# Spreading a phase's last products over the next phase's first, in a kernel of attention features and two feed-forward layers

## The chip, the cores and the metric

One core of a Trainium2 chip runs the program. The metric is the device time of one execution in microseconds. Three runs of the kernel before gave 2034.95, 2035.83 and 2037.15 us; their median is 2035.83 us. One further execution was profiled; it took 2038.37 us, of which the trace's span covers 2036.6 us.

## What is computed

```python
# attention with exponential features, then x of 2304 tokens x 512
x = np.ascontiguousarray(attn_out.transpose(0, 2, 1, 3)).reshape(B * S, H * D)
# layer 1: eight experts, all used by every token, weighted by P[:, e]
for e in range(E):                       # E = 8, w1[e] 512 x 1024, w2[e] 1024 x 512
    h = np.maximum(x @ w1[e], 0.0)
    out += P[:, e:e + 1] * (h @ w2[e])
# layer 2, on layer 1's output
h = np.maximum(np.maximum(x @ w1, x @ w2), x @ w3)      # each 512 x 768
return h @ w_out                                         # 768 x 512
```

P comes from a gate `exp(x @ w_gate)` with eight rounds of row and column normalisation. The second layer's weights arrive as 64-bit numbers and are made 32-bit on the chip ("wide" jobs).

## The kernel before

**Phases.** After the attention part the feed-forward part runs in four phases: phase 0 is layer 1 on the first half of the tokens (1152), phase 1 layer 1 on the second half, phases 2 and 3 are layer 2 on the first and the second half. A phase is a row of units of 256 hidden features: 32 units in a phase of layer 1, 3 in a phase of layer 2. A unit has one weight matrix m in layer 1 and three (m = 0, 1, 2) in layer 2. Each half has two token groups g = 0, 1 of 576 tokens.

**Products.** For each matrix and group, `group` (L304) computes the hidden block with seven products of half size. Product k multiplies a combination x0 to x6 of the input with a combination of the weight. They run in the order `PRODUCTS`, which asks for x0, x3, x4, x1, x5, x2, x6. Every product is six TensorE matmuls of 288 columns (L117 to L119), since each operand stands as a high and a low part. Three products' sums are copied from PSUM by ScalarE (u1, u5, u2: L354, L370, L374) and added on VectorE (L112, into ph or c); the third product x4 goes into the bank from which u1 was copied, x5 into the bank from which u2 was copied, x6 waits for the sum c. In layer 1 ScalarE applies the ReLU (h, L336) and VectorE makes the low part of h (L337). In layer 2 VectorE takes maxima in a tile d (L342), and with m = 2 ScalarE and VectorE write h from d (L344, L345).

**Tiles out.** `tile_out` (L386) multiplies 128 tokens of a unit's h with its second weight: six matmuls of 512 columns into a bank po or small, and one VectorE operation that adds into acc. A unit has nine tiles, t = 0 to 8. They are given between the products of the next unit's m = 0. After the last unit of a phase of layer 1, `retranspose` (L416) transposes each finished tile of acc on TensorE (four matmuls of 128 columns), ScalarE copies it (L422), and SP stores it in x_of for the phase two later.

**x jobs.** The next phase's x0 to x6 for a group are made by `x_jobs` (L133) from the group's x: four differences t3 to t6, seven high parts xh (ScalarE casts, L109), seven low parts xl (L112). `X_PLANS["between"]` says in `on` which engine makes high, low and t (A ScalarE, D VectorE, P GpSimd), and in `rest` their order. In the last group of a phase two jobs of the next phase's group 0 are issued with each product.

**At a phase's end** (L511 to L533) tiles 0 to 3 stand between the last products, tiles 4 to 8 follow in one piece with three x jobs behind each, and only then the next phase begins. Group 0's x is loaded into d, a tile of four parts that the wide jobs and the maxima use at other times; group 1's x is loaded into a buffer of h.

**Order.** The program is written in the order in which each engine runs it: there is no scheduler, and every engine takes its instructions in that order.

Of the kernel before, what the change touches and what calls it, by code (L numbers as in the profile page):

```python
# [29 lines left out]
    "between": dict(  # L30
        on=["ADD", "APD", "APD", "ADD", "ADD", "APD", "ADD"], early="h0 l0",
        rest="t3 h3 l3 t4 h4 l4 h1 l1 t5 h5 l5 h2 l2 t6 h6 l6", first=2, side=3, mix=1, weights="AAAA PPPP DDDD",
    ),
# [21 lines left out]
def tile_performer__moe__max3(ctx, tc, kq_t, kq, v1, omega2, w_gate, w1, w2, m1, m2, m3, m_out, out):  # L55
# [76 lines left out]

    def x_jobs(xf, g, plan, on=None):  # L133


        b11, b12 = xf[:, 0:2, 0:Q], xf[:, 0:2, Q:S]
        b21, b22 = xf[:, 2:4, 0:Q], xf[:, 2:4, Q:S]
        unmade.update((g, k) for k in range(7))
# [4 lines left out]
        def job(what, k):  # L143
            hi, lo = xo[g][k]
            if what == "t":
                src[k] = big.tile([P, 2, Q], F32, tag="t", name=f"t{k}", bufs=3)
                x, y = of[k]
                return lambda: tt(on[k][2], src[k], x, src[y] if isinstance(y, int) else y, ALU.subtract)
            if what == "h":
                return lambda: copy(on[k][0], hi, src[k])  # L150

            def low():
                tt(on[k][1], lo, src[k], hi.bitcast(F32), ALU.subtract)
                unmade.discard((g, k))
            return low
# [82 lines left out]

    def d4():
        return pools["b"].tile([P, KD, S], F32, tag="d", name="d")  # L240

    def wide_jobs(i, st):
# [3 lines left out]
        high = st.bitcast(I32).rearrange("p (f w) -> p f w", w=2)[:, :, 1]  # L246
        d = d4()
        sc, ma, fr = (d[:, j, :512] for j in range(3))
        sci, mai = sc.bitcast(I32), ma.bitcast(I32)
# [198 lines left out]
    def feed_forward():  # L448
        hs, last, tiles, x_plan = {}, None, [], X_PLANS["first"]
        for a, (u, m) in enumerate(mats):  # L450
            hf, layer, n = units[u]
# [3 lines left out]
            if m == 0:  # L455
                tiles += [(last, t) for t in range(HT)] if n else []
                h = hs[u] = new_h()
                hs.pop(u - 2, None)
                if layer == 2:
                    d = d4().rearrange("p k (g q) -> p k g q", g=G)  # L460
                    most[:] = [[d[:, 2 * i + j] for j in range(2)] for i in range(2)]
            if end:
# [3 lines left out]

            def load_x(out, g):
                nc.sync.dma_start(out=out, in_=x_of[phase + 1][:, :, g * S : (g + 1) * S])
                return out

            if more and layer == 1:
                xin = [load_x(d4(), 0)]
            if layer == 2 and m == 1 and n == FF2 // UF - 1 and phase < 3:
                xf = new_h(F32)
                xin = [load_x(xf[:, :, g * S : (g + 1) * S], g) for g in range(G)]

# [10 lines left out]

            def give_tile():  # L490
                v, t = tiles.pop(0)
                tile_out(v, hs[v], t)
                if v == u and layer == 1:
                    if t:
                        retranspose(2 + hf, t - 1)
                    if t == HT - 1:
                        retranspose(2 + hf, t)

            for g in range(G):
                own = end and g == G - 1  # L500
                if own:
                    while tiles:
                        give_tile()
                    if more:
                        if layer == 1:
                            xin.append(load_x(new_h(F32)[:, :, :S], 1))
                        side.extend(x_jobs(xin[0], 0, x_plan))
                pace = len(tiles)
                for i, _ in enumerate(group(a, g, h, PRODUCTS)):
                    piece()  # L510
                    if own and i == 2:  # L511
                        tiles = [(u, t) for t in range(HT // 2)]
                        pace = 0
                    if own:
                        if i > 2:
                            give_tile()
                    else:
                        left = pace - (i + 1) * pace // (7 if end else 7 * (G - g))
                        while len(tiles) > left:
                            give_tile()  # L520
                    yield
            while run_next(jobs):
                pass
            if end:
                while waiting:
                    one_more()
                if more:
                    side.extend(x_jobs(xin[1], 1, x_plan))
                tiles = [(u, t) for t in range(HT // 2, HT)]
                while tiles:  # L530
                    give_tile()
                    for _ in range(x_plan["side"]):
                        side_job()  # L533
            last = u


    def attention(pool, proj_pool):
# [167 lines left out]
        def X(s, part):  # L705
# [16 lines left out]
            if part == 1:  # L722
                if hp == HP - 1:
                    if hf == 0:
                        todo.extend(x_jobs(xf0[:, :, o : o + S], b, X_PLANS["first"], [ON["Jhi"] + ON["Jlo"] + ON["Jsum"]] * 7))
                    if b == G:
# [195 lines left out]
```

## Time and profile before

| | us |
|---|---|
| median of three runs | 2035.83 |
| profiled execution | 2038.37 |
| its span | 2036.6 |
| PE busy | 1972.6 (97%) |
| DVE busy | 1401.9 (69%) |
| ACT busy | 810.2 (40%) |
| POOL busy | 715.1 (35%) |
| phase 0 to 1, from the last group's first product to unit 1 | 918.5 to 963.6 |
| phase 1 to 2, to unit 0's second matrix | 1690.4 to 1735.5 |
| phase 2 to 3, to unit 0's second matrix | 1852.3 to 1897.9 |

PE is TensorE's matmul queue, DVE VectorE, ACT ScalarE, POOL GpSimd. Matmuls are pipelined: one of 288 columns is shown with about 0.30 us, but the next one starts 0.13 us later. So the cost of a matmul is read from start to start, and lost time is what lies above that.

### The profile page before, as it was taken

How to read it: one execution, taken by the hardware profiler on the slowest of the kernel's cores; microseconds unless marked ns; L12 is line 12 of the kernel's file. 1: busy time of each engine (PE TensorE's matmuls, PEld its weight loads, DVE VectorE, ACT ScalarE, POOL GpSimd, SP SyncE). 2: the span in 40 equal slices, each digit the busy share in tenths (PEclk: the TensorE clock that was granted, in tenths of full speed). 3: DMA queues.
4: the chain of work that ended last, by engine and by line, in shares of the span. 5: the costliest groups of instructions: out<-in, count | busy, mean ns of one | idle time of the engine just before them, and what ended most of it. 6: DMA issues, size and time to landing. Idle time of an engine off the chain costs nothing.

```text
span 2036.6 us, 33535 instructions
## 1 busy us (share of the span) xinstructions
PE 1972.6 (97%) x12906; PEld 1765.4 (87%) x12906; DVE 1401.9 (69%) x2741; ACT 810.2 (40%) x2011; POOL 715.1 (35%) x575
## 2 busy tenths in 40 slices
PE   8999999999999999998999999999999998998899
PEld 6778889999998998987999999999898987987888
DVE  5775778788878778766666666666666666567655
ACT  6775333333333333335333333333333334433442
POOL 2452234444434444423332222333222323333530
PEclk9999999999999999999999999999999999999999
DMA  6452112222222222213111111111111113113201
GB/s 206 151 187 71 42 47 73 94 80 82 73 73 73 82 90 83 68 45 112 52 46 49 42 42 42 42 52 53 42 42 42 42 65 103 51 32 120 67 22 47
DMA packets 92545, 143.95 MB, mean 71 GB/s; under 512 B 6496, under 2 KB 48608, under 8 KB 92384
## 3 DMA queue, kind: packets, MB, share of 16 engines
q1 hardware_dynamic: 92384, 141.81, 21.4%
q8 instruction: 101, 1.65, 0.3%
q14 instruction: 60, 0.49, 0.1%
HBM read 123.70 MB, written 18.09 MB: 70 GB/s over the span
## 4 chain that ended last, share of the span: by engine, by line
PE 89%; DVE 6%; ACT 3%; issue 1%; DMA 1%; SPq 0%; DVEq 0%; ACTq 0%
PE ph L117 15%; PE ph L118 14%; PE ph L119 14%; PE po L393 9%; PE po L394 9%; PE po L392 9%; PE small L393 5%; PE small L394 5%; PE small L392 5%; PE ph L621 1%; PE ph L565 1%; DVE small L624 1%; DVE s L112 1%; ACT qp L644 1%; DVE xl L112 1%
## 5 line engine op out<-in xcount | busy, mean ns | idle before, releaser
L117 PE MATMUL ph<-xh,wh 128*128 128x288 f32 x2296 | 688.8, 300 | 26.9 <-DVE c L112 10.3
L118 PE MATMUL ph<-xl,wh 128*128 128x288 f32 x2296 | 682.6, 297 | 0.0
L119 PE MATMUL ph<-xh,wl 128*128 128x288 f32 x2296 | 678.7, 296 | 0.0
L117 PEld LDWEIGHTS ph<-xh,wh 128*128 128x128 f32 x2296 | 434.7, 189 | 61.5 <-DVE c L112 14.0
L118 PEld LDWEIGHTS ph<-xl,wh 128*128 128x128 f32 x2296 | 435.0, 189 | 25.1
L119 PEld LDWEIGHTS ph<-xh,wl 128*128 128x128 f32 x2296 | 435.9, 190 | 0.0
L410 DVE SCALAR_TENSOR_TENSOR acc<-po,prob,acc 128x512 f32<-128x512 f32 x354 | 265.0, 748 | 203.0 <-PE po L394 200.9
L112 POOL TENSOR_TENSOR w2l<-st,w2h 128x512 fp32r<-128x512 f32 x140 | 183.7, 1333 | 621.8 <-ACT w2h L109 614.6
L336 ACT ACTIVATE h<-ph 128x288 fp32r<-128x288 f32 x384 | 157.8, 412 | 447.0 <-DVE ph L112 397.7
L392 PE MATMUL po<-w2h,h 128*128 128x512 f32 x834 | 328.2, 394 | 1.9 <-ACT h L344 1.9
L394 PE MATMUL po<-w2h,h 128*128 128x512 f32 x834 | 327.8, 393 | 1.8 <-DVE h L345 1.8
L393 PE MATMUL po<-w2l,h 128*128 128x512 f32 x834 | 328.9, 394 | 0.0
L112 POOL TENSOR_TENSOR wl<-st,wh 128x512 fp32r<-128x512 f32 (+1 forms) x162 | 168.0, 1043 | 292.4 <-ACT wh L109 292.4
L112 POOL TENSOR_TENSOR wl<-s,wh 128x512 fp32r<-128x512 f32 x162 | 213.6, 1323 | 31.2 <-ACT wh L109 28.6
L410 DVE SCALAR_TENSOR_TENSOR acc<-small,prob,acc 128x512 f32<-128x512 f32 x177 | 132.9, 751 | 121.7 <-PE small L394 120.9
L394 PEld LDWEIGHTS po<-w2h,h 128*128 128x128 f32 x834 | 157.1, 188 | 38.1 <-DVE h L345 2.7
L112 DVE TENSOR_TENSOR ph<-ph,u 128x288 f32<-128x288 f32 x304 | 140.3, 462 | 70.1 <-PE ph L119 54.6
L392 PEld LDWEIGHTS po<-w2h,h 128*128 128x128 f32 x834 | 157.1, 188 | 21.5 <-ACT h L344 2.3
L337 DVE SCALAR_TENSOR_TENSOR h<-ph,h 128x288 fp32r<-128x288 f32 x384 | 171.6, 447 | 2.0 <-ACT h L336 1.0
L393 PEld LDWEIGHTS po<-w2l,h 128*128 128x128 f32 x834 | 157.0, 188 | 18.3
L393 PE MATMUL small<-w2l,h 128*128 128x512 f32 x426 | 168.3, 395 | 0.0
L392 PE MATMUL small<-w2h,h 128*128 128x512 f32 x426 | 168.3, 395 | 0.0
(167 smaller groups left out, 2456.5 us busy)
## 6 DMA issues: line engine op xcount, KB each, us to landing
st<-in_moe_w_dram SPq DMA_DIRECT2D x146, 512.0 KB, 3.6
st<-plain SPq DMA_DIRECT2D x24, 512.0 KB, 3.7
raw<-in_kq_t_dram SPq DMA_DIRECT2D x15, 576.0 KB, 4.4
sq<-in_kq_dram SPq DMA_DIRECT2D x15, 576.0 KB, 5.0
plain<-d SPq DMA_DIRECT2D x24, 256.0 KB, 2.2
v<-in_v_dram SPq DMA_DIRECT2D x16, 325.0 KB, 5.1
h<-x_of SPq DMA_DIRECT2D x4, 1152.0 KB, 6.0
x_of<-xt SPq DMA_DIRECT2D x18, 256.0 KB, 2.6
```

The costliest lines, as they stand in the source:

```text
L112: (nc.gpsimd if on == "P" else nc.vector).tensor_tensor(out=out, in0=in0, in1=in1, op=op)
L117: nc.tensor.matmul(ps, wh, xh, start=start and not onto, stop=False, **given)
L118: nc.tensor.matmul(ps, wh, xl, start=False, stop=False, **given)
L119: nc.tensor.matmul(ps, wl, xh, start=False, stop=stop, **given)
L336: after(0, lambda: nc.scalar.activation(hh, c, AF.Relu))
L337: after(1, lambda: nc.vector.scalar_tensor_tensor(out=hl, in0=c, scalar=0.0, in1=hh.bitcast(F32), op0=ALU.max, op1=ALU.subtract))
L392: nc.tensor.matmul(ps, h[:, f, ts], wh[:, f], start=f == 0, stop=False)
L393: nc.tensor.matmul(ps, h[:, f, ts], wl[:, f], start=False, stop=False)
L394: nc.tensor.matmul(ps, h[:, 2 + f, ts], wh[:, f], start=False, stop=f == 1)
L410: nc.vector.scalar_tensor_tensor(out=a, in0=ps, scalar=prob[:, i, e : e + 1], in1=a, op0=ALU.mult, op1=ALU.add)
L565: nc.tensor.matmul(o[j], w[:, j], x, start=start, stop=stop)
L621: nc.tensor.matmul(ps[h][:, i], x[d, t0 + i], om[d, h * M : (h + 1) * M], start=True, stop=True)
```

## The change

Six things change.

1. The last unit's tiles 4 to 8 are no longer given in one piece. They stay in the list `tiles`, each with the transposition of the tile two before it, and are given between the next phase's first products. In phase 1 they are spread over both groups of its first unit.
2. In layer 2 a new function `due` spreads a unit's nine tiles over all its matrices, one behind the sixth product of each group and the rest evenly; before, all nine stood in m = 0. In the last unit of phase 2 they are spread over m = 0 and 1.
3. d becomes two tiles d0 and d1 of two parts each. At the change from phase 0 to 1 group 1's x is loaded into them, half by half, by the new jobs u0 and u1, once group 0's jobs have used the half. Elsewhere group 1's x still goes into a buffer of h, in two loads.
4. The x jobs between phases come in another order (t5 earlier), and the low part of x5 is made on VectorE instead of GpSimd: nine of the eleven differences and low parts of a group are now on VectorE, before eight.
5. In layer 2 the buffer h of a unit is taken with m = 2 instead of m = 0, and the next phase's x is loaded with the last unit's m = 2 instead of m = 1.
6. The x jobs of group 0 that are left at the phase's end, and all of group 1, run between the next phase's first products.

```diff
     "between": dict(
-        on=["ADD", "APD", "APD", "ADD", "ADD", "APD", "ADD"], early="h0 l0",
-        rest="t3 h3 l3 t4 h4 l4 h1 l1 t5 h5 l5 h2 l2 t6 h6 l6", first=2, side=3, mix=1, weights="AAAA PPPP DDDD",
+        on=["ADD", "APD", "APD", "ADD", "ADD", "ADD", "ADD"], early="h0 l0",
+        rest="t3 h3 t5 l3 u0 t4 h4 l4 h1 l1 t6 h2 l2 u1 h5 l5 h6 l6", first=2, side=3, mix=1, weights="AAAA PPPP DDDD",
     ),
...
+            if what == "u":
+                return lambda: used(k)
...
-    def d4():
-        return pools["b"].tile([P, KD, S], F32, tag="d", name="d")
+    def d2(c):
+        return pools["b"].tile([P, KD // 2, S], F32, tag=f"d{c}", name=f"d{c}")
...
+        def out_of(v):
+
+
+            hf, layer, n = units[v]
+            given = [[lambda t=t: tile_out(v, hs[v], t)] for t in range(HT)]
+            if layer == 1 and n == E * FF // UF - 1:
+                given += [[], []]
+                for t in range(HT):
+                    given[t + 2].append(lambda t=t: retranspose(2 + hf, t))
+            return given
+
...
+            if layer == 1 or m == 2:
+                hs.pop(u - 2, None)
                 h = hs[u] = new_h()
...
+            def used(c):
+                if phase == 0:
+                    xin[1].append(load_x(d2(c), 1, c))
...
+            def due(g, i):
+
+                if layer == 1:
+
+                    return pace - (i + 1) * pace // (7 if end else 7 * (G - g))
+
+                groups = G * (2 if end_unit and phase < 3 else 3)
+                q = G * m + g
+                rest = max(0, total - groups)
+                return max(0, total - q - (i >= 5) - min(rest, (7 * q + i + 1) * rest // (7 * groups)))
...
                     if own and i == 2:
-                        tiles = [(u, t) for t in range(HT // 2)]
-                        pace = 0
+                        tiles = out_of(u)
                     if own:
-                        if i > 2:
-                            give_tile()
+                        if 2 < i:
+                            give()
                     else:
-                        left = pace - (i + 1) * pace // (7 if end else 7 * (G - g))
+                        left = due(g, i)
                         while len(tiles) > left:
-                            give_tile()
+                            give()
                     yield
...
                 if more:
+                    while len(xin[1]) < 2:
+                        side_job()
                     side.extend(x_jobs(xin[1], 1, x_plan))
-                tiles = [(u, t) for t in range(HT // 2, HT)]
-                while tiles:
-                    give_tile()
-                    for _ in range(x_plan["side"]):
-                        side_job()
             last = u
+        while tiles:
+            give()
```

How it moves the instructions, at three places. In the names, xh03 is the high part of x3 of group 0 and xl13 the low part of x3 of group 1; wh0 and wl0 are the weight parts of one of two slots; `acc<-po,prob,acc` is a tile's addition.

On PE, the end of phase 0 in the kernel before: tile 8's last matmuls, the transpositions of tiles 7 and 8, and phase 1's first product.

```order
L392 MATMUL small_10228<-w2h_9864,h_9849 128x512
L393 MATMUL small_10228<-w2l_9865,h_9849 128x512
L394 MATMUL small_10228<-w2h_9864,h_9849 128x512
L420 MATMUL ph_10236<-ident_66,acc_2762 128x128 x4
L420 MATMUL ph_10244<-ident_66,acc_2762 128x128 x4
L117 MATMUL ph_10260<-xh00_68,wh0_100 128x288
L118 MATMUL ph_10260<-xl00_69,wh0_100 128x288
L119 MATMUL ph_10260<-xh00_68,wl0_101 128x288
```

In the changed kernel phase 1's products x0 and x3 come right behind tile 3 and the transposition of tile 1; behind them stand tile 4, the transposition of tile 2 and product x4:

```order
L394 MATMUL po_10202<-w2h_9890,h_9873 128x512
L395 MATMUL po_10202<-w2l_9891,h_9873 128x512
L396 MATMUL po_10202<-w2h_9890,h_9873 128x512
L422 MATMUL ph_10210<-ident_66,acc_2762 128x128 x4
L117 MATMUL ph_10174<-xh04_76,wh0_100 128x288
L118 MATMUL ph_10174<-xl04_77,wh0_100 128x288
L119 MATMUL ph_10174<-xh04_76,wl0_101 128x288
```

So five tiles and seven transpositions moved from ahead of phase 1's first product to places between its first fourteen.

On DVE, the same change of phase in the kernel before: group 0's last low part, then group 1's x jobs, taken from the buffer h, with the additions of the last tiles between them.

```order
L112 TENSOR_TENSOR xl06_81<-t6_10166,xh06_80 128x576
L112 TENSOR_TENSOR xl10_83<-h_10007,xh10_82 128x576
L410 SCALAR_TENSOR_TENSOR acc_2762<-po_10188,prob_67,acc_2762 128x512
L112 TENSOR_TENSOR t3_10204<-h_10007 128x576
L112 TENSOR_TENSOR xl13_89<-t3_10204,xh13_88 128x576
L410 SCALAR_TENSOR_TENSOR acc_2762<-po_10208,prob_67,acc_2762 128x512
L112 TENSOR_TENSOR t4_10224<-h_10007,t3_10204 128x576
L112 TENSOR_TENSOR xl14_91<-t4_10224,xh14_90 128x576
```

In the changed kernel:

```order
L112 TENSOR_TENSOR xl05_79<-t5_10068,xh05_78 128x576
L112 TENSOR_TENSOR xl06_81<-t6_10147,xh06_80 128x576
L112 TENSOR_TENSOR xl10_83<-d0_10080,xh10_82 128x576
L412 SCALAR_TENSOR_TENSOR acc_2762<-po_10202,prob_67,acc_2762 128x512
L112 TENSOR_TENSOR t3_10225<-d0_10080 128x576
L112 TENSOR_TENSOR t5_10228<-d1_10168,d0_10080 128x576
L112 TENSOR_TENSOR ph_10232<-ph_10232,u1_10171 128x288
L112 TENSOR_TENSOR xl13_89<-t3_10225,xh13_88 128x576
L112 TENSOR_TENSOR t4_10242<-d1_10168,t3_10225 128x576
```

The low part of x5 joined DVE's queue, group 1's x comes from d0 and d1, and a sum of phase 1's own first products (ph with u1) now stands among group 1's jobs.

On PE in phase 2, unit 0, m = 1, first group, the kernel before: product x2 is followed at once by product x6.

```order
L117 MATMUL ph_17636<-xh02_72,wh1_2493 128x288
L118 MATMUL ph_17636<-xl02_73,wh1_2493 128x288
L119 MATMUL ph_17636<-xh02_72,wl1_2494 128x288
L117 MATMUL ph_17626<-xh06_80,wh1_2493 128x288
L118 MATMUL ph_17626<-xl06_81,wh1_2493 128x288
L119 MATMUL ph_17626<-xh06_80,wl1_2494 128x288
```

In the changed kernel a tile and a transposition stand behind product x2, ahead of x6:

```order
L394 MATMUL po_17649<-w2h_17118,h_17101 128x512
L395 MATMUL po_17649<-w2l_17119,h_17101 128x512
L396 MATMUL po_17649<-w2h_17118,h_17101 128x512
L422 MATMUL ph_17657<-ident_66,acc_2762 128x128 x4
L117 MATMUL ph_17593<-xh06_80,wh1_2493 128x288
L118 MATMUL ph_17593<-xl06_81,wh1_2493 128x288
L119 MATMUL ph_17593<-xh06_80,wl1_2494 128x288
```

So a tile of six matmuls moved into a group that had none.

## Rows read from the trace of the kernel before

**Rows 1.** The page, busy time, share of the span and instructions by engine.

```profile
PE 1972.6 (97%) x12906; PEld 1765.4 (87%) x12906; DVE 1401.9 (69%) x2741; ACT 810.2 (40%) x2011; POOL 715.1 (35%) x575
```

**Rows 2.** Stretches: length, busy of PE, PEld, DVE, ACT, POOL; TensorE clock; DMA.

```profile
600.00:800.00 200.00, 200.00 (x1173) 180.36 (x1172) 160.26 (x290) 72.02 (x171) 84.01 (x68) 1.00 0.23 76
920.00:940.00 20.00, 18.45 (x109) 15.61 (x108) 15.46 (x24) 10.21 (x20) 4.26 (x3) 1.00 0.47 152
918.50:963.60 45.10, 37.79 (x218) 33.23 (x217) 30.80 (x50) 23.36 (x49) 16.07 (x12) 0.92 0.40 126
1690.40:1735.50 45.10, 37.51 (x219) 33.28 (x218) 30.09 (x45) 21.37 (x43) 16.43 (x12) 0.92 0.40 126
1852.30:1897.90 45.60, 33.84 (x179) 29.11 (x178) 34.39 (x53) 18.25 (x38) 20.69 (x16) 0.93 0.32 99
1735.50:1852.30 116.80, 112.00 (x743) 104.90 (x743) 70.10 (x145) 47.92 (x111) 41.03 (x33) 1.00 0.18 57
1897.90:2020.00 122.10, 117.65 (x779) 110.26 (x778) 72.10 (x150) 49.38 (x115) 40.15 (x32) 1.00 0.09 27
```

**Rows 3.** Timeline of PE, phase 0 to 1: start, duration, instruction, idle before.

```profile
945.10 0.66 PE L420 MATMUL ph<-ident,acc 128*128 128x128 f32 x4 [2.26 <-DVE acc L410]
946.28 0.44 PE L117 MATMUL ph<-xh,wh 128*128 128x288 f32 x1
946.52 0.44 PE L118 MATMUL ph<-xl,wh 128*128 128x288 f32 x1
955.12 0.40 PE L117 MATMUL ph<-xh,wh 128*128 128x288 f32 x1 [2.22 <-DVE c L112]
```

**Rows 4.** Timeline of PE, starts of a transposition, products and a tile.

```profile
929.74 0.60 PE L420 MATMUL ph<-ident,acc 128*128 128x128 f32 x4
930.10 0.38 PE L117 MATMUL ph<-xh,wh 128*128 128x288 f32 x1
...
964.39 0.29 PE L117 MATMUL ph<-xh,wh 128*128 128x288 f32 x1
...
965.19 0.39 PE L392 MATMUL po<-w2h,h 128*128 128x512 f32 x1
...
966.57 0.29 PE L117 MATMUL ph<-xh,wh 128*128 128x288 f32 x1
```

**Rows 5.** Timeline of DVE in the same stretch.

```profile
920.58 0.76 DVE L112 TENSOR_TENSOR xl<-d,xh 128x576 fp32r<-128x576 f32 x1 [0.74 <-ACT xh L109]
921.25 0.76 DVE L112 TENSOR_TENSOR t<-d 128x576 f32<-128x576 f32 x1
...
926.27 0.74 DVE L410 SCALAR_TENSOR_TENSOR acc<-po,prob,acc 128x512 f32<-128x512 f32 x1
926.93 0.45 DVE L112 TENSOR_TENSOR c<-ph,u 128x288 f32<-128x288 f32 x1
927.29 0.45 DVE L337 SCALAR_TENSOR_TENSOR h<-ph,h 128x288 fp32r<-128x288 f32 x1
...
950.21 1.52 DVE L112 TENSOR_TENSOR xl<-t,xh 128x576 fp32r<-128x576 f32 x1 [3.92 <-ACT xh L109]
```

**Rows 6.** Timeline of ACT in the same stretch.

```profile
947.24 0.40 ACT L354 COPY u<-ph 128x288 f32<-128x288 f32 x1 [0.24 <-PE ph L119]
947.53 0.68 ACT L109 CAST xh<-t 128x576 fp32r<-128x576 f32 x1
948.11 0.68 ACT L109 CAST xh<-h 128x576 fp32r<-128x576 f32 x1
```

**Rows 7.** Timeline of POOL, the operation that overlaps DVE's of 950.21.

```profile
949.83 1.28 POOL L112 TENSOR_TENSOR w2l<-st,w2h 128x512 fp32r<-128x512 f32 x1
```

**Rows 8.** Timeline of PE inside phase 2, stops with m = 1 and m = 2.

```profile
1741.12 0.40 PE L117 MATMUL ph<-xh,wh 128*128 128x288 f32 x1 [0.69 <-DVE c L112]
1756.57 0.40 PE L117 MATMUL ph<-xh,wh 128*128 128x288 f32 x1 [0.97 <-ACT u L354]
```

**Rows 9.** The page, DMA issues: count, size, median us to landing.

```profile
raw<-in_kq_t_dram SPq DMA_DIRECT2D x15, 576.0 KB, 4.4
```

## Prediction before the run

> **What bounds the kernel now.** I read the page first: PE is busy 97% of the span [rows 1], so time can only be won where PE stops or runs slowly. Then the stretches: from 600 to 800 us, inside phase 0, PE is busy for the whole 200 us at clock 1.00, and DVE has 20% to spare [rows 2]. At the three changes of phase it is not so: PE is busy 37.8, 37.5 and 33.8 us of some 45, and its clock is 0.92 to 0.93 on average. Inside phases 2 and 3 it is busy 112.0 of 116.8 and 117.65 of 122.1 us.
>
> What is lost there needs prices from start to start [rows 4]: a product takes 0.80 us (964.39 to 965.19), a tile 1.38, a transposition 0.36. The stretches of phase 0 to 1 and 1 to 2 hold 21 products, nine tiles and nine transpositions each: 16.8 + 12.4 + 3.2 = 32.4 us of 45.1, so 12.7 are lost. Phase 2 to 3 holds the same without transpositions: 29.2 of 45.6, 16.4 lost. Within this the clock accounts for about 0.08 x 45.1 = 3.6 us a change: after stops of 2.26 us the matmuls of 288 columns start 0.24 us apart instead of 0.13 [rows 3, 4], which is the lower of the two levels, 1.2 GHz; from 920 to 940 us PE was idle for 1.55 us and the clock stayed at 1.00 [rows 2]. The stops wait for DVE's addition ahead of a transposition, and then for the sum c ahead of x6, because DVE and ACT make the next phase's x at the same time [rows 3, 5].
>
> Inside phases 2 and 3 the idle time is 4.8 + 4.45 = 9.25 us [rows 2], in 16 stops of two kinds, x6 waiting for c and x4 waiting for the copy u1 [rows 8]. After each stop the first matmul is 0.10 us longer and the next one later, about 0.15 us a stop in all: 2.4 more, 11.7 lost. The four places together lose 12.7 + 12.7 + 16.4 + 11.7 = 53.5 us.
>
> **Tiles spread over the next phase, change 0 to 1.** I followed the new order by hand with DVE at 0.67 us for an operation of 576 columns, 0.66 for an addition into acc, 0.36 for one of 288 columns [rows 5], ACT at 0.58 for a cast of 576 columns and 0.29 for a copy u [rows 6]. Up to the next phase's x6, PE has 13 products, seven tiles and five transpositions from 918.5 us on: 10.4 + 9.7 + 1.8 = 21.9, so it arrives at 940.4. DVE, from its first x job at 920.6, has 14 operations of 576 columns, five additions, nine of 288 columns and one weight sum (about 0.5): 9.4 + 3.3 + 3.2 + 0.5 = 16.4 us, to 937.0. It also waits where a low part stands right behind its cast, 0.74 us in the row of 920.58; I find four such places, 0.4 to 1.2 us each, 3.3 together: 940.3, and the sum c stands there. So both queues arrive together, and PE stops for about 0.5 us. Later a transposition waits 0.8 for a bank that ACT has yet to copy out, and x4 of the second group 0.8 for u1, because ACT makes high parts ahead of it. That is 2.1 us. Ten hand-offs of 0.1 us that I did not count are 1.0 more.
>
> One cost is in no sum yet. The low part of 950.21 took 1.52 us instead of 0.76 [rows 5]; POOL was in an operation from 949.83 to 951.11 [rows 7]. So a meeting costs DVE 0.76 us. Between 935 and 951 us POOL has four operations in the new order, so at least nothing and at most 3.0 us; I take half, 1.5. Lost after the change: 2.1 + 1.0 + 1.5 = 4.6, gain 12.7 - 4.6 = 8.1.
>
> The Trainium skill (SBUF — State Buffer, section "SBUF: two separate sides") says that DVE and GpSimd share a pair of ports as an exclusive lock, so that a DVE operation with two inputs in SBUF waits until the GpSimd operation ends. The row of 950.21 agrees: 0.90 us were left of POOL's operation. By that rule the price of a meeting would lie between 0 and 1.28 us, on average 0.64, and the sum of four would be 2.6 in place of 1.5: a gain lower by 1.1 at each change.
>
> **The moved low part and the refill.** x5's low part costs DVE 0.67 us for each group, counted above. The second load of d0 is issued when t5 is done, 922.6 by my schedule, and used at 934; that of d1 waits for POOL's low part of x2, which ends at about 932.3, and on SP's queue a weight load and the later stores of x_of stand behind it. A load of this size took 4.4 us [rows 9], so it lands at 936.7, when DVE comes to t5 of group 1 at 936.9. I price it at nothing; each us that it is later is one us of DVE and of PE. The weight load behind it is used some 20 us later. The halves of d cost the wide jobs and the maxima nothing, since both halves are taken at once. The later load of phase 3's x has a whole group of 14 products in front of its use.
>
> **Change 1 to 2.** No h is computed with m = 0, so DVE is easier, and ACT is the late one: u2 stands behind two casts of weights, two high parts and u5, and PE waits 1.1 us with x5, 1.5 with x6 for DVE's sum, 1.5 and 1.4 in the second group. 5.5 in all, 1.5 for meetings and 0.5 for hand-offs: 7.5 instead of 12.7, gain 5.2. The three tiles and five transpositions left over take PE the same time later.
>
> **Change 2 to 3.** Tiles 4 to 8 no longer wait for the last h, so the stops for h are gone. By the same schedule PE waits 0.7 for u2 ahead of tile 1, 1.1, 1.6, 0.9 and 1.2 in phase 3's first products, and the stop of about 1.1 ahead of the stretch's third product stays, since no tile is left to stand in front of it: 6.6, with 1.5 and 0.5: 8.6 instead of 16.4, gain 7.8.
>
> **Inside phases 2 and 3.** A tile of 1.38 us now stands ahead of every x6, where the stops cost 0.4 to 0.85 us, and three products ahead of the x4 that waited 0.97 for u1 [rows 8]; DVE pays 0.66 for the tile in between, behind what x6 waits for. So the x6 stops go. The x4 stops go too, except in the first unit of each phase, where h's buffer is free only when the old phase's tile 8 is done: ACT's first cast of h waits for that, and the copies behind it with it, about 0.9 us left at either place. 11.7 - 1.8 - 0.4 (the last unit's group without a tile) = 9.5, and 0.5 off for new stops: 9.0. The bounds are 0, if ACT's order keeps PE waiting as now, and 11.7.
>
> **Sum.** 8.1 + 5.2 + 7.8 + 9.0 = 30.1 us. The profiled execution would go from 2038.37 to 2008.3 us; against the median of the runs, 2.5 us lower, from 2035.83 to 2005.7: I say 2006 us. If meetings and hand-offs cost nothing (4.5 and 2.0) and the inside gives all of its 11.7, it is 1997; with all meetings at their bound (4.5 more) and half of the inside, 2015.
>
> **Rivals.** First, DVE becomes the bound at the changes. For it: it would be busy some 30 of 36 us, and POOL works 16.07 of 45.1 us there [rows 2], so of 18 x operations on DVE about 6.4 meet one: 4.9 us instead of 1.5, and with stops that long the clock falls once a change, 1.8 us. 3 x (3.4 + 1.8) = 15.6 are lost again: 2021. Against it: most meetings now fall where PE has tiles to do. Chance 0.12.
>
> Second, ACT's order, not DVE's, sets the pace inside phases 2 and 3: the u copies stand behind casts that wait for DVE, and tiles in front only shift both. Then the 9.0 stay away: 2015. For it: the idle time of 0.97 names ACT [rows 8]. Against it: the tile is work of PE alone at that point. Chance 0.13.
>
> Third, the refill does not do what it says: d1 comes 4 us late behind the stores on SP's queue, and all of group 1's jobs with it: 2010. Chance 0.05, since a queue with this load is not in this trace.
>
> Fourth, the other side: slower. Stops of 1 to 1.6 us follow each other every third product in the first two groups of phases 1, 2 and 3, and the clock stays at its lower level through them. A product then takes 6 x 0.24 = 1.44 us, 0.64 more [rows 3], a tile about 1.1 more: 14 x 0.64 + 3 x 1.1 = 12.3 a phase, 37 for three, against 30 won: 2043. It decides from four fifths of these stretches at the lower level on. Against it: the clock is 1.00 on average in both stretches with stops of up to 0.97 us [rows 2, 8] and from 920 to 940 us with 1.55 us idle. Chance 0.03. I keep 0.05 for no change, if two of the rivals come together.
>
> **How the numbers follow.** The forecast has 0.62, the rivals 0.12, 0.13, 0.05 and 0.03, no change 0.05. The range from 1997 to 2020 holds nearly all of the forecast and the second and third rival, 0.79 with them. Within 0.2% of the time, 4 us, is what a measurement of this kernel can't tell from no change: faster 0.92, same 0.05, slower 0.03.
>
> **What would show it.** After the change the three stretches should show PE busy over 85% and the clock near 1.00; the stop ahead of phase 1's x6 should be under 1 us and name DVE's sum; no transposition should wait for acc in a row of its own; x6 inside phases 2 and 3 should not wait. If low parts on DVE last 1.3 us or more in numbers, the first rival is right; if PE's stops inside the phases still name u1, the second; if DVE's t5 of group 1 waits for a DMA, the third. The prediction is wrong if the time is above 2020 us, most of all if the clock shows 0.5 in several rows of one change.

## The result, and the profile after

The changed kernel takes 2014.07 us (median of four runs, 2012.78 to 2014.88), the kernel before, run beside it, 2035.39 us: a ratio of 0.9893, interval 0.9876 to 0.9910, so 21.3 us faster. The forecast was 2006 us, within 1997 to 2020. The sign and the range held; the gain was 8 to 9 us smaller than the sum said. The profiled execution took 2014.74 us, its span is 2012.9.

The page answers to [rows 1]:

```profile
PE 1964.0 (98%) x12906; PEld 1758.5 (87%) x12906; DVE 1413.4 (70%) x2747; ACT 807.7 (40%) x2011; POOL 710.6 (35%) x569
```

The stretches answer to [rows 2], with the same columns: the three changes of phase, each from the last group's first product to the point 21 products later, and between them the insides of phases 2 and 3 (the last to the last matmul).

```profile
914.40:952.10 37.70, 35.52 (x218) 31.76 (x216) 33.28 (x53) 22.47 (x49) 14.63 (x10) 0.95 0.32 95
1678.70:1714.30 35.60, 29.78 (x179) 26.57 (x178) 31.21 (x44) 18.16 (x38) 15.62 (x10) 0.95 0.32 100
1714.30:1832.90 118.60, 117.03 (x779) 109.69 (x778) 72.84 (x148) 49.70 (x117) 40.11 (x33) 1.00 0.22 68
1832.90:1873.30 40.40, 30.38 (x164) 25.92 (x164) 36.55 (x52) 18.23 (x39) 18.94 (x14) 0.92 0.28 91
1873.30:2008.70 135.40, 132.98 (x854) 123.06 (x852) 83.27 (x168) 50.18 (x118) 40.08 (x32) 1.00 0.15 50
```

The first change is as forecast, with PE busy for 94% of it. The second, at 84%, just misses the 85% that the prediction named as its sign. The third misses it clearly: PE is busy for 75%, and DVE for 36.55 of 40.4 us. Nor is the clock near 1.00 at the changes: in this profile it stood at 0.50 from 944.4 to 947.8, from 1709.0 to 1712.4 and from 1866.0 to 1872.8 us.

**One measure for all runs.** The loss of a stretch is its length less what its matmuls cost from start to start, by the medians over all matmul records of the kernel before: 0.133 us for 288 columns, 0.231 for 512, 0.109 for a transposition's 128. Change 2 to 3 after: 21 products of six and six tiles of six are 16.8 + 8.3 = 25.1, of 40.4 us, so 15.3 are lost (15.4 before rounding). The prediction's count by [rows 4] took a transposition at 0.36 instead of 0.44, began the last stretch 0.4 us later, and had 12.7, 12.7 and 16.4 for the kernel before; by this one they are 11.9, 11.8 and 16.8. The losses of all kernels, in us (inside is phases 2 and 3 beyond the changes, to the last matmul):

| kernel | 0→1 | 1→2 | 2→3 | inside | sum | median |
|---|---|---|---|---|---|---|
| before | 11.9 | 11.8 | 16.8 | 15.7 | 56.2 | 2035.4 |
| after | 4.5 | 8.8 | 15.4 | 8.2 | 36.8 | 2014.1 |
| e1, tiles not spread in layer 2 | 2.9 | 2.5 | 12.1 | 15.1 | 32.6 | 2012.0 |
| e2, POOL's work at the changes left out | 0.7 | 4.5 | 5.6 | 8.1 | 18.9 | 1996.5 |
| e3, POOL's work at the changes on DVE | 3.4 | 5.7 | 9.3 | 8.4 | 26.8 | 2005.4 |
| e4, left-over tiles in m = 0 | 2.9 | 2.5 | 12.1 | 12.4 | 30.0 | 2008.9 |
| e5, left-over tiles in one piece | 8.9 | 11.0 | 17.1 | 12.3 | 49.3 | 2025.2 |
| e6, low part of x5 on POOL | 5.2 | 7.1 | 13.6 | 8.2 | 34.1 | 2011.2 |
| e7 = e3 + e4 | 3.4 | 1.3 | 7.9 | 12.7 | 25.3 | 2005.3 |
| e8 = e4, weights alone on DVE | 3.6 | 1.4 | 8.2 | 12.3 | 25.5 | 2004.2 |
| e9 = e4, x alone on DVE | 4.1 | 3.5 | 11.0 | 12.4 | 31.0 | 2009.4 |
| e10 = e8, weights earlier | 4.5 | 0.8 | 7.3 | 11.9 | 24.5 | 2002.8 |
| e11 = e10, weights behind the x jobs | 3.2 | 1.1 | 6.4 | 11.9 | 22.5 | 2001.0 |
| e12 = e11, low part of x5 on POOL | 2.1 | 1.0 | 6.9 | 12.1 | 22.0 | 2000.6 |

The median less the sum lies between 1975.9 and 1980.0 us in every row. So these four places account for the time of all fourteen kernels, to about 2 us. A loss is read from one profiled execution, and it holds what the clock did in that one: change 0 to 1 is the same work in the changed kernel, e1 and e4, and lost 4.5 us with the clock at 0.95, 2.9 and 2.9 with it at 1.00. Differences of up to some 1.6 us between two rows can therefore be the clock's.

### The profile page after: what moved, and what is told of

It reads as the page before. It is cut to its first block, busy times and chain, and to the rows that moved or that the text cites. A ratio compares the mean times of both kernels' runs of the same rounds, so it can differ in the third digit from the quotient of the medians.

```text
span 2012.9 us, 33562 instructions
## 1 busy us (share of the span) xinstructions
PE 1964.0 (98%) x12906; PEld 1758.5 (87%) x12906; DVE 1413.4 (70%) x2747; ACT 807.7 (40%) x2011; POOL 710.6 (35%) x569
## 4 chain that ended last, share of the span: by engine, by line
PE 90%; DVE 5%; ACT 2%; issue 1%; DMA 0%; SPq 0%; DVEq 0%; ACTq 0%
PE ph L117 14%; PE ph L118 14%; PE ph L119 14%; PE po L395 9%; PE po L394 9%; PE po L396 9%; PE small L395 5%; PE small L394 5%; PE small L396 5%; PE ph L654 1%; PE ph L598 1%; ACT qp L677 1%; DVE small L657 1%; PE ph L699 1%; DVE s L112 1%
```

## Where the gain went

The stops of PE in change 2 to 3 of the changed kernel: start, duration, instruction, and in brackets the idle time before and what ended it. Three of the ten.

```profile
1854.19 0.40 PE L118 MATMUL ph<-xl,wh 128*128 128x288 f32 x1 [1.71 <-DVE xl L112]
...
1865.55 0.40 PE L117 MATMUL ph<-xh,wh 128*128 128x288 f32 x1 [1.98 <-ACT u L376]
1866.86 0.61 PE L118 MATMUL ph<-xl,wh 128*128 128x288 f32 x1 [0.91 <-DVE xl L112]
```

Behind the last one the clock is at its lower level: from 1867.26 the matmuls of 288 columns start 0.24 us apart, until 1872.46. The timeline of DVE at the same place, and that of POOL:

```profile
1862.79 1.39 DVE L112 TENSOR_TENSOR t<-h,t 128x576 f32<-128x576 f32 x1
1864.11 1.49 DVE L112 TENSOR_TENSOR s<-st,s 128x256 f32<-128x256 f32 x1
1865.52 3.03 DVE L112 TENSOR_TENSOR xl<-t,xh 128x576 fp32r<-128x576 f32 x2
```

```profile
1860.57 3.00 POOL L112 TENSOR_TENSOR xl<-h,xh 128x576 fp32r<-128x576 f32 x2 [7.42 <-ACT xh L109]
1863.53 2.66 POOL L112 TENSOR_TENSOR wl<-st,wh 128x512 fp32r<-128x512 f32 x2
1866.15 3.55 POOL L112 TENSOR_TENSOR wl<-s,wh 128x512 fp32r<-128x512 f32 x2
```

From 1860.57 to 1869.70 POOL never stops, and DVE's operations last 1.4 to 1.5 us each; the last PE row above waits for such an xl. The first PE row waits for an xl of usual length, but it stood behind two low parts of h that were stretched to 1.3 us each beside POOL:

```profile
1850.83 2.63 DVE L347 TENSOR_TENSOR h<-d,h 128x288 fp32r<-128x288 f32 x2
1853.39 1.41 DVE L112 TENSOR_TENSOR xl<-t,xh 128x576 fp32r<-128x576 f32 x2
```

```profile
1850.42 2.73 POOL L112 TENSOR_TENSOR w2l<-st,w2h 128x512 fp32r<-128x512 f32 x2 [0.73 <-ACT w2h L109]
```

No stop of PE in the three stretches names POOL itself; all name DVE or ACT. That a stretched DVE, not a lack of work beside it, costs PE its time is one theory; the other is that too few tiles stand between the first products of phases 2 and 3, since the spread of part 2 gives only one tile to a group there. The experiments measure both; their expectations call the first "meetings" (of a DVE operation with one of POOL) and the second "cover".

## Experiments

**e1: the spread of layer 2's tiles undone.**

```diff
             def due(g, i):
-                if layer == 1:
+                if True:
```

> The changed kernel, with the tiles of layer 2 back in the first matrix (m = 0) of each unit, as before; all else of the change stays. My theory: the spread of layer 2's tiles is worth the 7.2 us that PE loses less inside phases 2 and 3, so these stops return: 2021 us, loss inside the phases back from 7.6 to about 14 us, the stops ahead of x6 naming the sum c. Rival: ACT's order, not the missing tile, sets those stops; then the time stays within 2 us of the changed kernel's 2014. A second point: with all of the five left-over tiles in the first two groups of phase 3, the change 2 to 3 has more work for PE in it; if these tiles are what it lacks, its loss falls from 15.4 to 11 us or less, and the total is 2016 to 2018.

Measured: 2012.01 us, ratio 0.9881 (0.9867 to 0.9896). The stops inside came back as forecast, 8.2 to 15.1 us, yet the time did not rise. It is the time that the rival expected, but not for its reason: 1 to 2 lost 2.5 instead of 8.8 us, and 2 to 3 12.1 instead of 15.4. The windows of its three changes:

```profile
916.00:952.10 36.10, 33.92 (x218) 30.33 (x216) 33.18 (x53) 22.35 (x49) 14.61 (x10) 1.00 0.33 96
1678.70:1714.30 35.60, 33.89 (x216) 30.42 (x215) 33.09 (x49) 20.34 (x43) 15.29 (x10) 1.00 0.42 129
1830.60:1871.90 41.30, 34.57 (x182) 29.55 (x182) 37.65 (x53) 18.61 (x40) 19.00 (x14) 0.92 0.22 77
```

Change 1 to 2 takes the same 35.6 us as after and holds three tiles and five transpositions more. Cover is a real part of the loss at 1 to 2; at 2 to 3 it leaves 12.1 us. The change 0 to 1, whose instructions are those of the changed kernel, lost 2.9 instead of 4.5: its clock is 1.00 here instead of 0.95.

**e2: POOL's work at the changes left out.** The low parts that POOL would make while x jobs are pending are not made; old values stand in their place, for the second weight its high part.

```diff
-        on=["ADD", "APD", "APD", "ADD", ...], ... weights="AAAA PPPP DDDD",
+        on=["ADD", "A-D", "A-D", "ADD", ...], ... weights="AAAA ---- DDDD",
...
     def tt(on, out, in0, in1, op):
+        if on == "-":
+            return
...
```

> The changed kernel without GpSimd's work at the changes of phase: the low parts of x1 and x2 and the low parts of the weights made while x jobs are pending are not made (old values stand in their place). VectorE, ScalarE and TensorE keep all their instructions. Theory 'meetings': VectorE is late at the changes because its operations are stretched while GpSimd works (about 5, 7 and 9 us of excess at the three changes); then losses fall from 4.5, 8.8 and 15.4 us to about 3, 4 and 8, 28.7 to 15 in all: 2000 us. Rival 'cover': too few tiles stand between the first products of phases 2 and 3, so TensorE runs ahead of the x jobs anyway; then the losses fall by under 4 us in all: 2010 us or more.

Measured: 1996.47 us, ratio 0.9804 (0.9789 to 0.9819); 0.7, 4.5 and 5.6 us lost, 10.8 against 28.6. That is more than the theory of meetings expected. Its three windows:

```profile
914.50:948.30 33.80, 33.36 (x216) 30.31 (x215) 28.51 (x53) 22.28 (x49) 0.00 (x0) 1.00 0.36 106
1675.00:1706.30 31.30, 27.97 (x180) 25.17 (x179) 24.62 (x44) 18.10 (x38) 0.00 (x0) 1.00 0.35 114
1824.80:1855.40 30.60, 26.62 (x163) 23.42 (x163) 26.16 (x51) 18.23 (x39) 0.00 (x0) 1.00 0.36 120
```

With the same 53 and 44 instructions, and 51 instead of 52, DVE is busy 28.51, 24.62 and 26.16 us instead of 33.28, 31.21 and 36.55: POOL stretched it by 4.8, 6.6 and 10.4 us. PE lost 3.8, 4.3 and 9.8 us by it, the lower clock included: the clock is 1.00 in all three windows here. Of the 3.8 at the first change some 1.6 are the clock's fall, which e1 and e4 don't have in the same work. Which operations stretch is seen in the groups of DVE by form (count, busy, mean ns), in change 2 to 3 of the changed kernel

```profile
L347 DVE TENSOR_TENSOR h<-d,h 128x288 fp32r<-128x288 f32 x8 | 8.2, 1034 | 0.0
L112 DVE TENSOR_TENSOR xl<-t,xh 128x576 fp32r<-128x576 f32 x8 | 7.5, 952 | 0.1
L112 DVE TENSOR_TENSOR t<-h,t 128x576 f32<-128x576 f32 x4 | 4.8, 1197 | 0.0
...
L405 DVE TENSOR_TENSOR acc<-po,acc 128x512 f32<-128x512 f32 x4 | 2.7, 680 | 0.0
L112 DVE TENSOR_TENSOR d<-ph,u 128x288 f32<-128x288 f32 x6 | 2.6, 447 | 0.7 <-PE ph L119 0.7
```

and in this experiment:

```profile
L114 DVE TENSOR_TENSOR xl<-t,xh 128x576 fp32r<-128x576 f32 x8 | 6.0, 756 | 0.8 <-ACT xh L109 0.6
L350 DVE TENSOR_TENSOR h<-d,h 128x288 fp32r<-128x288 f32 x8 | 3.5, 451 | 0.0
L114 DVE TENSOR_TENSOR t<-h,t 128x576 f32<-128x576 f32 x4 | 3.0, 750 | 0.0
...
L408 DVE TENSOR_TENSOR acc<-po,acc 128x512 f32<-128x512 f32 x4 | 2.7, 684 | 0.0
L114 DVE TENSOR_TENSOR d<-ph,u 128x288 f32<-128x288 f32 x6 | 2.7, 456 | 1.0 <-PE ph L121 1.0
```

The low part of h goes from 451 to 1034 ns, t from 750 to 1197, xl from 756 to 952. What reads a bank of PSUM (po, ph) does not move: 684 and 680, 456 and 447. Against the durations of this run, 6, 8 and 11 of DVE's operations at the three changes of the changed kernel are over 0.15 us longer, by 4.6, 6.8 and 9.6 us together: 0.77 to 0.87 us each. In the kernel before they were 4, 6 and 10. The Trainium skill (SBUF — State Buffer, section "SBUF: two separate sides") states that the port pair shared by DVE and GpSimd is an exclusive lock, taken by DVE operations with two inputs in SBUF; the rows agree in which forms are stretched and which are not.

**e3: the same work on DVE instead.**

```diff
-        on=["ADD", "APD", "APD", "ADD", ...], ... weights="AAAA PPPP DDDD",
+        on=["ADD", "ADD", "ADD", "ADD", ...], ... weights="AAAA DDDD DDDD",
...
-            ... else loaders[kind][1](i, st)
+            ... else w2_jobs(i, st, "A" + on.split()[1][0]) if kind == "w2" else wide_jobs(i, st)
```

> The changed kernel with the same GpSimd work of the changes made on VectorE instead. VectorE gets four low parts of x at 0.67 us, four low parts of weights and two of the second weight at about 0.55, some 6 us a change more, and loses what GpSimd's operations stretch. Theory 'meetings': the stretch of 5, 7 and 9 us is as much as the added work, so the time is within 4 us of 2014, with the change 2 to 3 better (15.4 to 12 us lost) and the change 0 to 1 no better. Rival 'load': VectorE's own count of operations is the bound and the meetings cost little; then each change loses 4 to 6 us more: 2027 us.

Measured: 2005.43 us, ratio 0.9849 (0.9834 to 0.9864), better than either theory. The windows of its changes:

```profile
914.20:950.70 36.50, 34.29 (x216) 30.27 (x215) 33.41 (x61) 21.45 (x46) 0.00 (x0) 1.00 0.33 98
1678.20:1710.70 32.50, 28.11 (x179) 25.08 (x178) 30.05 (x54) 18.03 (x38) 0.00 (x0) 1.00 0.34 110
1829.20:1863.60 34.40, 28.66 (x165) 24.88 (x164) 33.17 (x65) 18.22 (x40) 0.00 (x0) 0.95 0.31 107
```

DVE does 8, 10 and 13 instructions more and is busy 33.41, 30.05 and 33.17 us, about as long as after at the first change and less at the other two. So GpSimd's share of the work gave nothing here.

**e4: the left-over tiles in the first matrix.** Only unit 0 of phases 2 and 3 is given its tiles as phase 1 does it.

```diff
-                if layer == 1:
+                if layer == 1 or n == 0:
```

> The changed kernel, with the tiles left over from the old phase all given in the first matrix of phases 2 and 3, evenly over its two groups as phase 1 does it; the later units keep the spread. Theory 'cover': the losses at 1 to 2 and 2 to 3 fall by 4 us each, and four to eight stops of 0.5 us ahead of x6 return in the matrices m = 1 and 2 of those units: about 2009 us. Rival 'meetings': VectorE is late whatever TensorE has to do, and the additions of the tiles come on top (three or four at 0.66 us): 2014 to 2017 us.

Measured: 2008.86 us, ratio 0.9863 (0.9846 to 0.9879), as the theory of cover had it: 2.5 at 1 to 2, 12.1 at 2 to 3, and 4.2 us more inside. So both causes are real. At 1 to 2 cover, taken alone, is worth 6.3 us and meetings, taken alone, 4.3; at 2 to 3 cover 3.3, meetings 9.8. They overlap: 6.3 and 4.3 are more than the 8.8 lost at 1 to 2.

**e5: the left-over tiles in one piece at a phase's end.** Behind the last group:

```diff
+                while tiles:
+                    give()
+                    for _ in range(x_plan["side"]):
+                        side_job()
             last = u
```

> The changed kernel, with the tiles that are left at a phase's end again given in one piece, three x jobs behind each, before the next phase starts; the spread of layer 2's tiles, the two halves of d and the plan stay. My theory: at the change 0 to 1 the spread is what cut the loss from 11.9 to 3 to 4.5 us, so 8 us come back there; at 1 to 2 and 2 to 3 the loss returns to about 12 and 17 us: 2014 + 8 + 3 + 1.5 = 2026 us. Rival: the new plan of x jobs and the earlier load into d gave part of the gain at 0 to 1, and that part stays: 2020 us or less, with under 8 us lost at 0 to 1.

Measured: 2025.24 us, ratio 0.9951 (0.9938 to 0.9965). That is what the theory expected (2026). Spreading these tiles is worth some 11 us of the change's 21, by the losses 8.3 at the changes and 4.1 inside. At 0 to 1 it lost 8.9, not 12: about 3 us of the gain there belong to the plan, d's halves and the earlier load together, which this run doesn't separate.

**e6: the low part of x5 on POOL.**

```diff
-        on=["ADD", "APD", "APD", "ADD", "ADD", "ADD", "ADD"]
+        on=["ADD", "APD", "APD", "ADD", "ADD", "APD", "ADD"]
```

> The changed kernel with the low part of x5 back on GpSimd; the order of jobs stays. Theory 'meetings': a low part on GpSimd takes 1.4 us there and stretches what VectorE does beside it by about as much as the 0.67 us that VectorE saves; the time is within 3 us of the changed kernel's 2014, rather above it. Rival 'load': VectorE's own count is the bound; each change has 2 x 0.67 = 1.3 us less to do, 4 us in all: 2010 us.

Measured: 2011.24 us, ratio 0.9882 (0.9869 to 0.9896), an interval that overlaps the changed kernel's. By the losses it is 1.7 us better at each of the two later changes and 0.7 worse at the first: between the theories. At 1 to 2 that can be the clock, 1.00 here and 0.95 in the changed kernel; on the other side PE waits 1.15 and 0.84 us at the two later changes for POOL's low part of x5 itself. The ninth job on DVE was not what gave the change its gain.

**e7 to e9: both edits, and the halves of the split.** e7 is e3 and e4 together; e8 leaves x1 and x2 on POOL and moves the weights' low parts; e9 the reverse.

> The changed kernel with both edits that helped in the first runs: GpSimd's work at the changes on VectorE, and the left-over tiles of the first unit of phases 2 and 3 all in its first matrix. Theory: the two causes (VectorE stretched by GpSimd, too few tiles beside the x jobs) are separate and their gains of about 8.6 and 5.2 us add: 2000 us, with 2 to 3 us lost at 0 to 1 and at 1 to 2 and 6 to 7 at 2 to 3. Rival: tiles and low parts both need VectorE in the same stretch, and the gains overlap: 2004 us or more, with over 4 us lost at 1 to 2.

> As the run before, but the low parts of x1 and x2 stay on GpSimd, so only the weights' low parts move to VectorE at the changes. Theory 'meetings': what counts is any GpSimd operation in the stretch; four of the ten stay, 5.7 us of GpSimd a change, and stretch VectorE by about half of it, while VectorE has 2.7 us less to do: about the same time as the run before, within 3 us. Rival: only the weights' operations matter, since they lie where VectorE makes the last low parts: 2 to 3 us a change better than the run before.

> The other half of the split: the left-over tiles in the first matrix, the low parts of x1 and x2 moved to VectorE, the low parts of weights left on GpSimd. With both moved, TensorE lost 3.4, 1.3 and 7.9 us at the changes, with the weights alone moved 3.6, 1.4 and 8.2, with neither 2.9, 2.5 and 12.1. Theory: any GpSimd operation beside VectorE's x jobs costs alike, so moving the four low parts of x gives about half of the 3 to 4 us at 2 to 3: 2006 us, 10 us lost there. Rival: only the weights' operations count, and VectorE just gets more work: 2009 us or more, 12 us or more lost at 2 to 3.

Measured: e7 2005.32 us, 0.9851 (0.9836 to 0.9867); e8 2004.24, 0.9848 (0.9834 to 0.9861); e9 2009.37, 0.9871 (0.9857 to 0.9884). e7 did not add: the changes fall to 12.6 us, and the stops inside take 4.3 back, as the rival said of the total, though not of the place (1 to 2 lost 1.3, not over 4). Tiles covered stops that e3 had already removed: alone they take 9.6 us off the two later changes, on top of e3 5.8. e8 is as good as e7, as its theory said, and e9 no better than e4 (17.5 us at the changes there, 18.6 here), so the gain lies in moving the weights. The windows of change 2 to 3 in e4, e8 and e9:

```profile
1829.20:1870.50 41.30, 33.17 (x182) 28.19 (x181) 37.71 (x53) 18.70 (x41) 19.06 (x14) 0.96 0.28 96
1827.00:1864.40 37.40, 32.37 (x182) 27.99 (x182) 35.60 (x63) 18.64 (x40) 5.86 (x4) 0.95 0.30 99
1829.70:1869.90 40.20, 32.59 (x182) 28.30 (x181) 37.54 (x57) 18.69 (x40) 15.03 (x10) 0.96 0.28 98
```

Ten operations of the weights moved to DVE, at 0.62 us each there (e8), leave it busy 2.1 us less; four of x, at 0.75 each (e9), leave it busy 0.2 us less. For each operation taken from POOL the stretch of DVE falls by about 0.8 us in both. So a low part of x doesn't meet DVE less than one of a weight; moved, it costs DVE about what it saves, and there are fewer of them. That the weights come in a train behind two of x (the POOL rows above) may add to it, but these runs don't show it.

**e10 to e12: the weights moved out of the way.** In e10 the last matrix of a phase runs its weight jobs at double pace, in its first group and on POOL; in e11 the next phase's first matrix also starts its own only when no x job is left; e12 is e11 with the low part of x5 on POOL.

```diff
-            jobs = weight_jobs(a + 1, x_plan["weights"] if side or end else X_PLANS["first"]["weights"])
+            jobs = weight_jobs(a + 1, x_plan["weights"] if side else X_PLANS["first"]["weights"])
-            per = -(-sum(... for kind, _ in plan[a + 1]) // 14)
+            per = -(-sum(... for kind, _ in plan[a + 1]) // (7 if more else 4 if side else 14))
...
-        ... mix=1, weights="AAAA DDDD DDDD",
+        ... mix=0, weights="AAAA DDDD DDDD",
```

> As the kernel with only the weights' low parts on VectorE at the changes and the left-over tiles in the first matrix; here the weights for the next phase's first matrix are also finished in the first group of the last matrix, by GpSimd, before the x jobs begin. VectorE then has four low parts of 0.3 to 0.6 us and some weight sums less in the last group. Theory: VectorE is full at 2 to 3 (no gap from 1828 to 1861 in the kernel with all on VectorE), so its 8.2 us lost there fall by 2 to 3 and the others by up to 1: 2000 us. Rival: the stops move to the group before, whose matrices have little beside them in layer 2: 2004 us, the same.

> As the run before, and in the next phase's first matrix the weight jobs wait until the x jobs are all issued. Theory: the last x jobs of group 1 come earlier by the 4 to 5 us of weight work on VectorE that stood among them, so x6 of the second group finds its input: 1 to 2 us less lost at each change, 1996 us. Rival: the weights are then late for the second matrix, and TensorE waits for them at its first products: 2003 us or more.

> As the run before (2001 us; 3.2, 1.1 and 6.4 us lost at the changes), with the low part of x5 back on GpSimd, so that six low parts of x a change, three a group, are GpSimd's and no weights are. Theory 'load': with no weights on GpSimd there, a low part of x that it takes saves VectorE 0.67 us and meets little; 2 to 3 loses 1.5 us less, the others about the same: 1999 us. Rival 'meetings': the third low part follows right behind the second and stretches VectorE by over a microsecond each time: 2002 us or more, over 4 us lost at 0 to 1.

Measured: e10 2002.82 us, 0.9840 (0.9827 to 0.9853); e11 2000.96, 0.9832 (0.9818 to 0.9845); e12 2000.55, 0.9830 (0.9813 to 0.9848). The intervals of e8, e10 and e11 overlap, and e10 and e11 lie between theory and rival: each took 0.9 us off change 2 to 3, less than expected there. e11 and e12 beat both kernels, by some 13 us the changed one; they can't be told apart, and e12's expectations missed both ways (0 to 1 better by 1.1, 2 to 3 worse by 0.5). Change 2 to 3 of e11:

```profile
1824.80:1860.40 35.60, 31.18 (x183) 26.75 (x182) 35.08 (x58) 17.73 (x37) 9.23 (x7) 1.00 0.30 110
```

DVE is busy for 35.08 of 35.6 us. What is left there, 6.4 us, is DVE's work and still some meetings: POOL is busy for 9.23 us beside it, and the last low parts of x take 1.33 us each again:

```profile
1851.47 2.66 DVE L112 TENSOR_TENSOR xl<-t,xh 128x576 fp32r<-128x576 f32 x2
```

```profile
1849.51 3.34 POOL L112 TENSOR_TENSOR xl<-h,xh 128x576 fp32r<-128x576 f32 x2 [9.31 <-ACT xh L109]
```

## Why the prediction was right or wrong

**What bounds the kernel** was right: time can only be won where PE stops, and the losses carry the time of every run.

**Change 0 to 1** was forecast to gain 8.1 and gained 7.4 us in the profile. The three stops it named are there:

```profile
937.40 0.40 PE L117 MATMUL ph<-xh,wh 128*128 128x288 f32 x1 [0.46 <-DVE c L112]
942.67 0.66 PE L422 MATMUL ph<-ident,acc 128*128 128x128 f32 x4 [1.21 <-ACT xt L424]
943.84 0.40 PE L117 MATMUL ph<-xh,wh 128*128 128x288 f32 x1 [0.51 <-ACT u L356]
```

They were forecast at 0.5, 0.8 and 0.8. But the agreement of the sum is partly luck: without POOL 0.7 us is lost, not the 3.1 of stops and hand-offs, and POOL cost 3.8, not 1.5. Of the 3.8 some 1.6 are the fall of the clock behind the last two stops, for which the sum had no term; in e1 and e4 the same three stops came without it.

**The term that failed is the price of meetings**: 1.5 us at each change, half of four meetings of 0.76. The price of one, from [rows 5], was fair: the stretched operations are 0.77 to 0.87 us longer. The number was not: 6, 8 and 11 are stretched, where the sum paid for two at each change. The rows of the changes show 10, 10 and 14 operations on POOL (some in trains without a gap), and it is not only the x jobs that meet them but also weight sums and, at 2 to 3, five of the eight low parts of h. The trace of the kernel before, with 4, 6 and 10 stretched, could have warned of it. Measured by e2: 3.8 + 4.3 + 9.8 = 17.9 us instead of 4.5. By the rule of the Trainium skill (SBUF — State Buffer, section "SBUF: two separate sides") the prediction would have put it at 7.8 (three times 2.6): nearer, and short by the same wrong count.

**Change 2 to 3** (forecast 7.8, measured 1.4) is this term almost alone. The stops worked out by hand, 6.6 and 0.5, stand against 5.6 without POOL; the rest is the 9.8 that POOL costs there, the lower clock from 1866.0 to 1872.8 included. **Change 1 to 2** (5.2 forecast, 3.1 measured) has 4.3 for meetings instead of 1.5, and 4.5 instead of 6.0 for the rest. That its stops of 5.5 stand close to the 5.8 us that PE was idle there is luck: they were worked out without POOL's stretch, and without POOL it is 3.3.

**Inside phases 2 and 3** the gain was 7.5, forecast 9.0. One stop in each phase still names u1, in the first unit as forecast, of 0.48 and 0.44 us instead of 0.9. That the x6 stops go was only partly right: with m = 1 and 2 one of 0.22 us is left, but three new ones of about 0.6 us stand ahead of x6 with m = 0 in the later units, where the kernel before had none, and wait for DVE's sum d. The first of them:

```profile
1751.10 0.40 PE L117 MATMUL ph<-xh,wh 128*128 128x288 f32 x1 [0.61 <-DVE d L112]
```

The step that is missing is the price of the tiles moved there. "PE the same time later" is right for their own time, but they had covered DVE's work at the changes: e1 shows the spread gaining 6.9 us inside and costing 9.6 at 1 to 2 and 2 to 3. Part 2 of the change is worth nothing by itself; in the later units alone (e4) it is worth about 3 us (12.4 against 15.1 inside).

**The balance** in losses: 13.4 more for meetings, 1.5 less gained inside and 1.2 from the other count of the kernel before make 16.1; 5.4 that the hand schedule had set too high (3.1 + 6.0 + 7.1 against 10.8) come off: 10.7 us, which is 30.1 less the measured 19.4. The medians moved by 21.3, 1.9 more than the losses.

**The refill** cost nothing, as priced. The second load of d1 was issued at 928.80, a load of d in this stretch took 3.9 us, and t5 of group 1 starts on DVE without a wait:

```profile
928.80 0.37 SPq L484 DMA_DIRECT2D d<-x_of  x1
```

```profile
d<-x_of SPq DMA_DIRECT2D x2, 576.0 KB, 3.9
```

```profile
933.53 0.74 DVE L112 TENSOR_TENSOR t<-d,d 128x576 f32<-128x576 f32 x1
```

The slack is 0.8 us by these rows, so the third rival was close without being true.

**Rivals.** The first (2021 us, all meetings paid, chance 0.12) had the mechanism: its 4.9 us a change stand against 3.8, 4.3 and 9.8, its sign came at 2 to 3 (low parts of 1.3 us or more), and the clock fell once at each change, as it said. Its time was missed because the rest was cheaper. The second, ACT's order inside phases 2 and 3, did not come: 7.5 of the 9.0 us were gained there, and only the two stops of 0.48 and 0.44 us still name u1. At the changes ACT is named at many stops; taking POOL's work away shortens some of them (at 2 to 3 the longest from 1.98 to 0.71 us) and leaves others (0.92 and 0.95 at 1 to 2), so ACT's order may be part of what is lost there; no run changed it. The fourth did not come either: the longest time at the lower clock at a change is the 6.8 us from 1866.0 to 1872.8.

## What to carry to other kernels

Count in the trace at hand what another engine's operations meet before work is packed beside them: the same stretch with that engine's work left out gives the price in one run, and moving the work to the engine that it disturbs can be cheaper than sharing. A tile or any block of pure TensorE work is worth most where the other engines are late; before it is spread evenly, ask what it covered where it stood.

## What was not expected of the hardware

Two engines that share work gave less than one: DVE did 13 instructions more at 2 to 3 in e3 and was busy for 33.17 us, against 36.55 beside POOL. DVE is stretched in the steady part of phase 0 too, where PE is busy for the whole 200 us and it costs nothing: between 600 and 800 us of the changed kernel the low part of h takes 447 ns from PSUM and 899 from c in SBUF, with the same shape; without POOL, at e2's change 0 to 1, it takes 450 from c.

```profile
L339 DVE SCALAR_TENSOR_TENSOR h<-ph,h 128x288 fp32r<-128x288 f32 x51 | 22.8, 447 | 0.2
...
L339 DVE SCALAR_TENSOR_TENSOR h<-c,h 128x288 fp32r<-128x288 f32 x17 | 15.3, 899 | 0.0
```

And the attention part, which the change does not order anew, takes from 153.5 to 158.8 us with the granted clock between 0.99 and 0.95. Of the kernel before and of e12:

```profile
4.00:162.80 158.80, 144.39 (x2013) 115.06 (x2013) 108.83 (x339) 110.43 (x374) 67.74 (x42) 0.95 0.53 172
```

```profile
4.00:157.50 153.50, 139.21 (x2013) 110.62 (x2013) 109.05 (x340) 110.88 (x376) 67.80 (x42) 0.99 0.54 178
```

That is 5 us between two profiled executions, as much as some edits here are worth, and why stretches of the same instructions were compared rather than whole times. What decides it was not tried.
